# Attention, feed-forward and gated attention: separate PSUM banks for the row maxima of the first batch

## The chip, the cores and the metric

The kernel runs on one core of a Trainium2 chip. Its metric is the device time of one execution in microseconds (us); the kernel before took 964.29 us, the median of three runs (964.15 to 964.66). The profiled execution took 960.93 us, of which 959.20 us are the span from the first instruction to the last.

## The reference

Three stages follow each other on 4 batches of 576 tokens. First a causal attention with 8 heads of 64 and a decay per token:

```
scores = scale * (q @ k.T) + decay;  masked above the diagonal
scores = scores - max(scores, axis=-1)
attn   = exp(scores) / (sum(exp(scores)) + 1e-9)
x      = attn @ v                                   # heads side by side: 576 x 512
```

Then a mixing along the tokens and a feed-forward part with 2048 hidden units:

```
u  = x + (x.T @ U @ V).T
x  = u + relu(u @ w_ch1) @ w_ch2
```

The third stage is attention again, with four experts as heads and a gate that keeps two of them per token. The change lies in the first stage only.

## The kernel before, in words

The eight heads of a batch are worked on in four pairs; 16 pairs in all, numbered 0 to 15 in the code (`p`). The first batch, pairs 0 to 3, has the chip to itself; from pair 4 on (`later_batches`) matmuls of the feed-forward part are put between the attention's by a fixed pattern. A matmul in single precision is made of two or three products of rounded parts.

For each head, `row_max` forms the scores once with rounded operands, in two tiles of two PSUM banks each: `ua` (the last 128 rows, two matmuls) and `ub` (the other rows, four matmuls). VectorE (DVE) reduces both to the maximum of each row (`junk`, `mx`). A small product on TensorE (PE) turns the column `mx` into rows (`mt`), DVE copies it out (`mr`), and two DMAs on SyncE's queue (SP) write it as one more row of the operand `qa`. So `scores` yields differences to the maximum by itself: tile `sc`, two halves of two banks each. ScalarE (ACT) takes the exponential (`pf`) and rounds it (`ph`), DVE forms the rest (`pl`), and `weighted_values` multiplies with the values into one bank (`av`). DVE divides (`den`, `rn`, `x`). The maxima of pair p+1 are formed during pair p.

`value_scale` finds the largest value of a pair through two small products, `amt` and `rsp`. `mix` forms `gp` from the pair's result, ACT and DVE copy it out as `g`, and two products `up` are copied by ACT into `ustage` and sent to memory (`udram`). The feed-forward part loads them again (`ust`), rounds them on ACT (`uh`) and GpSimd (POOL, `ul`), and forms `hps` (hidden) and `cps` (output).

The weights `w1` and `w2` come in tiles: a DMA (`raw`), one step on DVE (L303), one on ACT (L304), two on DVE (L305, L306) into `wst`, then the rounded part on ACT (`w1h`, `w2h`) and the rest on POOL (`w1l`, `w2l`). `load_pair` reads the inputs `qkt` and `vr`; ACT and POOL round them, and SP copies them between partitions.

PSUM has eight banks. Three pools share them: `ps2`, two buffers of two banks (`ua`, `ub` and `sc` take turns in them); `ps1`, one bank (`av`); `psf`, three banks for all small products and the feed-forward products.

What sets the order: from pair 4 on PE's order is the one the code is written in. Everywhere else, and on all other engines, a scheduler orders the instructions before the run from its own estimate of when a buffer comes free; each engine, and SP's queue, then runs its list strictly in that order.

Of the kernel before, what the change touches and what calls it, by code (L numbers as in the profile page):

```python
# [8 lines left out]
F32 = mybir.dt.float32  # L9
# [8 lines left out]
P = 128  # L18
# [4 lines left out]
R = 32  # L23
NP = H // 2
NT = 5
SP_ = 640
HC = 288
# [29 lines left out]
def kernel(  # L57
# [16 lines left out]
    PSUM = bass.MemoryType.PSUM  # L74
# [8 lines left out]
    const = pool("const")  # L83
    dram = pool("dram", space=bass.MemoryType.DRAM)
    ps2 = pool("ps2", 2, space=PSUM)
    ps1 = pool("ps1", 1, space=PSUM)
    psf = pool("psf", 3, space=PSUM)
    small = pool("small", 4)


# [40 lines left out]
    ydram = dram.tile([B, P, KT, S], F32, name="ydram")  # L131
    cdram = dram.tile([B * H, 2, S], F32, name="cdram")

    cur = {}
    counter = [0]


# [10 lines left out]
    def row_max(hb, mx):  # L148


        qa, qb, ka, kb = hb
        ua = ps2.tile([P, 2, 512], F32, name="ua", tag="s2")
        for c0, c1 in ((0, HC), (HC, S)):
            nc.tensor.matmul(ua[:, c0 // HC, 0:HC], qa[0:66, M_LO[4]:S], ka[0:66, c0:c1],
                             start=True, stop=True)
        ub = ps2.tile([P, 2, 512], F32, name="ub", tag="s2")
        where = {3: (0, 0), 0: (0, 448), 2: (1, 0), 1: (1, 320)}
        for t in (3, 2, 1, 0):
            bk, off = where[t]
            w = M_W[t]  # L160
            n = 64 if t == 0 else P
            nc.tensor.matmul(ub[0:n, bk, off:off + w], qa[0:66, M_LO[t]:M_LO[t] + n],  # L162
                             ka[0:66, 0:w], start=True, stop=True)
        junk = cur["att"].tile([P, S], BF16, name="junk", bufs=1)
        nc.vector.tensor_tensor_reduce(
            junk[:].rearrange("p (c n) -> p c n", c=2), ua[:, :, 0:HC],
            maskm[:].rearrange("p (c n) -> p c n", c=2), 1.0, NEG, OP.add, OP.max, mx[:, 4:5])
        for t in (3, 2, 1, 0):
            bk, off = where[t]
            w = M_W[t]  # L170
            n = 64 if t == 0 else P
            m0 = S - P if t == 0 else S - w
            nc.vector.tensor_tensor_reduce(  # L173
                junk[0:n, 0:w], ub[0:n, bk, off:off + w], maskm[0:n, m0:m0 + w], 1.0, NEG,
                OP.add, OP.max, mx[0:n, t:t + 1])
        yield
        mt = psf.tile([NT, P], F32, name="mt", tag="f")
        nc.tensor.transpose(mt[:], mx[:], ident[:])
        mr = small.tile([NT, P], F32R, name="mr", bufs=2)
        nc.vector.tensor_scalar(mr[:], mt[:], PSCALE_LN / ISC, None, OP.subtract)  # L180
        row = f32(qa[66:67, :])
        nc.sync.dma_start(row[:, 0:64], f32(mr[0:1, 0:64]))
        return nc.sync.dma_start(row[:, 64:S].rearrange("o (t p) -> o t p", p=P),
                                 f32(mr[1:NT, :]))
# [59 lines left out]
    def value_scale(vr):  # L244

        am = small.tile([P, 1], F32, name="am")
        nc.vector.tensor_reduce(am[:], vr, AX.XYZ, OP.max, apply_absolute_value=True)
        yield
        at_ = psf.tile([1, P], F32, name="amt", tag="f")
        nc.tensor.transpose(at_[:], am[:], ident[:])  # L250
        ar = small.tile([1, 1], F32, name="ar")
        nc.vector.tensor_reduce(ar[:], at_[:], AX.X, OP.max)
        nc.vector.tensor_scalar(ar[:], ar[:], 1.0e-30, None, OP.max)
        nc.vector.tensor_scalar(ar[:].bitcast(I32), ar[:].bitcast(I32), 0x7F800000, None,
                                OP.bitwise_and)
        yield

        rp = psf.tile([P, 1], F32, name="rsp", tag="f")
        nc.tensor.matmul(rp[:], ones1[:], ar[:].bitcast(BF16)[:, 1:2], start=True, stop=True)
        rs = small.tile([P, 1], F32, name="rs")  # L260
        nc.vector.reciprocal(rs[:], rp[:])
        return rs
# [95 lines left out]

    def ffn_hidden(t, weights, uh, ul):
        w1h, w1l, w2h, w2l = weights  # L360
        ph = psf.tile([P, HC], F32, name="hps", tag="f")
        fs = slice(t * P, t * P + P)
        todo = [(w, uh, k) for k in range(KT) for w in (w1h, w1l)]
        todo += [(w1h, ul, k) for k in range(KT)]
        for n, (wa, xa, k) in enumerate(todo):
            nc.tensor.matmul(ph[:], wa[:, k, fs], xa[:, k, :], start=n == 0,  # L366
                             stop=n == 3 * KT - 1)
        hh = cur["fh"].tile([P, HC], F32R, name="hh")
        hl = cur["fh"].tile([P, HC], F32R, name="hl")
        nc.scalar.activation(hh[:], ph[:], AF.Relu)  # L370
        nc.vector.scalar_tensor_tensor(hl[:], ph[:], 0.0, f32(hh[:]), OP.max, OP.subtract)  # L371
        return hh, hl

    def ffn_out(d, weights, hs, yc):
        w1h, w1l, w2h, w2l = weights
        pc = psf.tile([P, HC], F32, name="cps", tag="f")
        dsl = slice(d * P, d * P + P)
        n = 0
        for t, (hh, hl) in enumerate(hs):
            for wa, xa in ((w2h, hh), (w2l, hh), (w2h, hl)):  # L380
                nc.tensor.matmul(pc[:], wa[:, t, dsl], xa[:], start=n == 0, stop=n == 3 * FT - 1)  # L381
                n += 1
        nc.vector.tensor_tensor(yc[:, d, :], pc[:], yc[:, d, :], OP.add)  # L383
# [158 lines left out]
    def mix(p):  # L542

        b, m, x = p // NP, p % NP, xs[p]
        gp = psf.tile([3 * R, P], F32, name="gp", tag="f")
        for t in range(NT):
            k = 64 if t == NT - 1 else P
            nc.tensor.matmul(gp[:], ut[0:k, t, :], x[0:k, t, :], start=t == 0,  # L548
# [4 lines left out]
        yield  # L553
        ust = sx.tile([P, S], F32, name="ustage")
        for (t0, t1, c0, c1) in ((0, 2, 0, 256), (2, 5, 256, S)):
            up = psf.tile([P, 512], F32, name="up", tag="f")
# [98 lines left out]
    def later_batches():  # L655
# [4 lines left out]
        for p in range(NP, NPAIR):  # L660
# [30 lines left out]
            if p == NP:  # L691
                sin0.release()
                att0.release()
                pre.release()
                cur["fu"] = pool("fu", 2, "right")
                cur["fh"] = pool("fh", 8, "right")
                cur["fy"] = pool("fy", 3, "right")
# [116 lines left out]
    def project(w0, y):  # L814

        yh, yl = y
        for c in range(NC):
            pq = psf.tile([P, HC], F32, name="pq", tag="f")
            cs = slice(c * HC, c * HC + HC)
            n = 0  # L820
            for k in range(KT):
# [33 lines left out]
    def expert_values(b, y):  # L855
# [2 lines left out]
        vr = sy.tile([P, NT, NV], F32, name="vr3", bufs=1)  # L858
        v0 = 2 * E * D
        for t in range(NT):  # L860
            pv = psf.tile([P, 512], F32, name="pv", tag="f")
            ts_ = slice(t * P, t * P + P)
            n = 0
            for k in range(KT):
# [15 lines left out]
    def turn_outputs(b, m, oh, ol):  # L880
# [2 lines left out]
        ms = slice(m * P, m * P + P)  # L883
        for (t0, t1) in ((0, 3), (3, 5)):
            c0, c1 = t0 * P, min(t1 * P, S)
            op = psf.tile([P, 512], F32, name="op", tag="f")
# [8 lines left out]
    def out_products(t, oh, ol, which):  # L895
        k = 64 if t == NT - 1 else P
        ts_ = slice(t * P, t * P + k)
        po = psf.tile([P, 512], F32, name="po", tag="f")
# [68 lines left out]
    with tc.manual_schedule(engines={mybir.EngineType.PE}):  # L967
# [46 lines left out]
                work_on(2 if more else 1)  # L1014
        expert_attend(B - 1, E - 1)
        work_on(100)
    for p_ in (ys[1], sy, att, hpool2, hpool, sy0, sw, small, psf, ps1, ps2, dram, const):
        p_.release()


# [55 lines left out]
```

## Time and profile before

| | |
|---|---|
| median of 3 runs | 964.29 us |
| profiled execution | 960.93 us, span 959.20 us |
| PE busy | 862.3 us (90% of the span) |
| DVE, ACT, POOL busy | 554.7, 416.5, 286.7 us |
| mean granted TensorE clock | 0.944 of full speed |

Busy time is the time in which an engine has an instruction running; the rest is waiting. The profile says for each wait which engine or DMA ended it. The granted clock is 1.00 at 2.4 GHz and 0.50 at 1.2 GHz. A line such as L218 is a line of the kernel before; in the changed kernel the same line stands two further down in the first stage.

### The profile page before, as it was taken

To read this page: it belongs to the slowest core of one execution; us is meant where nothing else is said; L and a number is where in the kernel's file an instruction comes from. 1 tells how busy PE (TensorE), PEld (TensorE's weight loads), DVE (VectorE), ACT (ScalarE), POOL (GpSimd) and SP (SyncE) were. 2 spreads that over 40 slices of the span, in tenths; PEclk is the share of its full clock that TensorE was granted. 3 is DMA by queue.
4 is the path that set the end of the run, shared out by engine and by line. 5 is a ranking of instruction groups with operands and counts; after the bars stand their busy time and mean duration, and the time that the engine had idled before them with its cause. 6 is when DMAs were issued, how large, how long until landed. Compare 5 with 4: busy or idle time off the path is not lost.

```text
span 959.2 us, 19001 instructions
## 1 busy us (share of the span) xinstructions
PE 862.3 (90%) x7480; PEld 804.7 (84%) x7480; DVE 554.7 (58%) x1468; ACT 416.5 (43%) x784; POOL 286.7 (30%) x238
## 2 busy tenths in 40 slices
PE   4887778989999989989999999999999787999987
PEld 3766567888888878989999999999998787888965
DVE  7787677877666555542255652222225566667674
ACT  4556455655445544442134442222113444545454
POOL 8445354443433224021135333323023303001010
PEclk9987568999999999999999999999999787999999
DMA  6434454444533332103168653424006210212201
GB/s 172 136 84 133 146 155 140 120 133 130 138 108 84 104 109 60 52 14 112 50 222 286 217 203 111 149 73 127 28 26 183 65 40 12 75 38 65 49 36 66
DMA packets 68777, 101.94 MB, mean 106 GB/s; under 512 B 6608, under 2 KB 49424, under 8 KB 68688
## 3 DMA queue, kind: packets, MB, share of 16 engines
q1 hardware_dynamic: 64416, 92.47, 32.7%
q10 hardware_dynamic: 4272, 8.26, 2.3%
q8 instruction: 59, 0.97, 0.4%
q14 instruction: 30, 0.25, 0.1%
HBM read 60.33 MB, written 22.56 MB: 86 GB/s over the span
## 4 chain that ended last, share of the span: by engine, by line
PE 67%; DVE 12%; DMA 8%; ACT 6%; issue 4%; POOL 2%; SPq 1%; ACTq 0%; POOLq 0%; DVEq 0%
PE hps L366 19%; PE cps L381 18%; PE sc L209 8%; PE pq L823 4%; PE pv L866 3%; DMA ust<-udram 2%; DVE pl L220 2%; PE po L901 2%; PE av L236 2%; PE gp L548 2%; PE ub L162 2%; ACT pf L218 2%; DVE junk L173 2%; PE av L240 2%; PE av L238 2%
## 5 line engine op out<-in xcount | busy, mean ns | idle before, releaser
L381 PE MATMUL cps<-hh,w2h 128*128 128x288 f32 x512 | 156.3, 306 | 5.6 <-DVE yc L383 3.7
L381 PE MATMUL cps<-hh,w2l 128*128 128x288 f32 x512 | 153.1, 299 | 1.3 <-POOL w2l L341 1.3
L381 PE MATMUL cps<-hl,w2h 128*128 128x288 f32 x512 | 152.2, 297 | 0.0
L220 DVE TENSOR_TENSOR pl<-pf,ph 128x576 f16<-128x576 f32 x144 | 117.7, 823 | 51.8 <-ACT ph L219 51.2
L366 PE MATMUL hps<-uh,w1h 128*128 128x288 f32 x512 | 145.3, 305 | 0.2 <-ACT uh L351 0.2
L366 PE MATMUL hps<-uh,w1l 128*128 128x288 f32 x512 | 141.8, 299 | 0.0
L371 DVE SCALAR_TENSOR_TENSOR hl<-hps,hh 128x288 fp32r<-128x288 f32 x128 | 58.0, 453 | 119.1 <-ACT hh L370 119.0
L370 ACT ACTIVATE hh<-hps 128x288 fp32r<-128x288 f32 x128 | 52.3, 409 | 155.1 <-PE hps L366 154.9
L218 ACT ACTIVATE pf<-sc 128x576 f32<-128x576 f32 x144 | 84.0, 612 | 61.3 <-PE sc L209 55.9
L381 PEld LDWEIGHTS cps<-hh,w2h 128*128 128x128 f32 x512 | 97.9, 191 | 6.5 <-DVE yc L383 4.4
L381 PEld LDWEIGHTS cps<-hh,w2l 128*128 128x128 f32 x512 | 97.9, 191 | 1.5 <-POOL w2l L341 1.5
L366 PEld LDWEIGHTS hps<-uh,w1h 128*128 128x128 f32 x512 | 97.9, 191 | 0.6 <-ACT uh L351 0.4
L366 PEld LDWEIGHTS hps<-uh,w1l 128*128 128x128 f32 x512 | 97.9, 191 | 0.0
L381 PEld LDWEIGHTS cps<-hl,w2h 128*128 128x128 f32 x512 | 97.7, 191 | 0.0
L236 PE MATMUL av<-vh,ph 128*128 128x65 f16 x720 | 91.9, 206 | 1.9 <-DVE x L282 1.6
L366 PE MATMUL hps<-ul,w1h 128*128 128x288 f32 x512 | 89.4, 297 | 4.6 <-POOL ul L352 4.6
L238 PE MATMUL av<-vl,ph 128*128 128x64 f16 x720 | 90.5, 202 | 0.0
L240 PE MATMUL av<-vh,pl 128*128 128x65 f16 x720 | 90.0, 202 | 0.1
L209 PE MATMUL sc<-qa,ka 67*128 67x288 f32 (+4 forms) x288 | 83.0, 348 | 7.9 <-ACT pf L218 3.8
L219 ACT CAST ph<-pf 128x576 f16<-128x576 f32 x144 | 88.3, 638 | 1.6
L236 PEld LDWEIGHTS <-ph 128*128 128x128 f16 x720 | 70.9, 104 | 13.7 <-issue 5.6
L173 DVE CUSTOM_DVE_ANT_0 junk<-ub,maskm 128x448 bf16<-128x448 f32 x192 | 79.6, 414 | 3.2 <-PE ub L162 1.2
(160 smaller groups left out, 1966.1 us busy)
## 6 DMA issues: line engine op xcount, KB each, us to landing
raw<-in_w_dram SPq DMA_DIRECT2D x32, 512.0 KB
ust<-udram SPq DMA_DIRECT2D x22, 576.0 KB
qkt<-in_qk_dram SPq DMA_DIRECT2D x16, 576.0 KB
yc<-ydram SPq DMA_DIRECT2D x14, 576.0 KB
ydram<-yc SPq DMA_DIRECT2D x14, 576.0 KB
vr<-in_v_dram SPq DMA_DIRECT2D x16, 320.0 KB
udram<-ustage ACTq DMA_DIRECT2D x16, 288.0 KB
ydram<-ust SPq DMA_DIRECT2D x8, 576.0 KB
```

Of the source, the lines that this page charges most:

```text
L173: nc.vector.tensor_tensor_reduce(junk[0:n, 0:w], ub[0:n, bk, off:off + w], maskm[0:n, m0:m0 + w], 1.0, NEG, OP.add, OP.max, mx[0:n, t:t + 1])
L209: nc.tensor.matmul(ps[:, bk, off:off + w], wa, xa, start=bk not in banks[:n], stop=bk not in banks[n + 1:])
L218: nc.scalar.activation(pfv, view, AF.Exp, scale=ISC)
L219: nc.scalar.copy(ph[:, o0:o0 + n], pf[:, 0:n])
L220: nc.vector.tensor_tensor(pl[:, o0:o0 + n], pf[:, 0:n], ph[:, o0:o0 + n], OP.subtract)
L236: nc.tensor.matmul(av[0:m, it, :], ph[0:k, c:c + m], vh[0:k, jt, :], start=first, stop=False)
L238: nc.tensor.matmul(av[0:m, it, 0:64], ph[0:k, c:c + m], vl[0:k, jt, :], start=False, stop=False)
L240: nc.tensor.matmul(av[0:m, it, :], pl[0:k, c:c + m], vh[0:k, jt, :], start=False, stop=last)
L366: nc.tensor.matmul(ph[:], wa[:, k, fs], xa[:, k, :], start=n == 0, stop=n == 3 * KT - 1)
L370: nc.scalar.activation(hh[:], ph[:], AF.Relu)
L371: nc.vector.scalar_tensor_tensor(hl[:], ph[:], 0.0, f32(hh[:]), OP.max, OP.subtract)
L381: nc.tensor.matmul(pc[:], wa[:, t, dsl], xa[:], start=n == 0, stop=n == 3 * FT - 1)
```

## The change

The pool `psf` with three banks is replaced, until the middle of pair 4, by two pools: `psm` with one buffer of two banks, which `ua` and `ub` share, and `psg` with one bank, which all small products share. `ps2` is left to the scores alone. In the middle of pair 4 both pools are released, `ua` and `ub` go back to `ps2`, and `psf` is made with three banks as before.

```
+    psm = pool("psm", 1, space=PSUM)
+    psg = pool("psg", 1, space=PSUM)
-    psf = pool("psf", 3, space=PSUM)
...
-    cur = {}
+    cur = {"psm": psm, "psf": psg}
...
-        ua = ps2.tile([P, 2, 512], F32, name="ua", tag="s2")
+        ua = cur["psm"].tile([P, 2, 512], F32, name="ua", tag="s2")
...
-        ub = ps2.tile([P, 2, 512], F32, name="ub", tag="s2")
+        ub = cur["psm"].tile([P, 2, 512], F32, name="ub", tag="s2")
...
-        mt = psf.tile([NT, P], F32, name="mt", tag="f")
+        mt = cur["psf"].tile([NT, P], F32, name="mt", tag="f")
...
                 pre.release()
+                psg.release()
+                psm.release()
+                cur["psm"] = ps2
+                cur["psf"] = pool("psf", 3, space=PSUM)
```

Every other use of `psf` becomes `cur["psf"]` in the same way. No instruction is added or removed; with other buffers the scheduler puts them in another order on every engine.

On PE, at the start of the kernel, the list of the kernel before (`ka0`, `qa0` are the first head of pair 0, `ka1` the second, `ka2` the first head of pair 1):

```order
L154 MATMUL ua_214<-ka0_138,qa0_136 128x288 x2
L162 MATMUL ub_217<-ka0_138,qa0_136 128x448
L162 MATMUL ub_217<-ka0_138,qa0_136 128x320
L162 MATMUL ub_217<-ka0_138,qa0_136 128x192
L162 MATMUL ub_217<-ka0_138,qa0_136 64x64
L154 MATMUL ua_234<-ka1_146,qa1_144 128x288 x2
L178 MATMUL mt_228<-ident_72,mx1_94 5x128
L162 MATMUL ub_237<-ka1_146,qa1_144 128x448
L162 MATMUL ub_237<-ka1_146,qa1_144 128x320
L162 MATMUL ub_237<-ka1_146,qa1_144 128x192
L162 MATMUL ub_237<-ka1_146,qa1_144 64x64
L154 MATMUL ua_312<-ka2_154,qa2_152 128x288 x2
```

The same place in the changed kernel:

```order
L156 MATMUL ua_217<-ka0_141,qa0_139 128x288 x2
L164 MATMUL ub_220<-ka0_141,qa0_139 128x448
L164 MATMUL ub_220<-ka0_141,qa0_139 128x320
L164 MATMUL ub_220<-ka0_141,qa0_139 128x192
L164 MATMUL ub_220<-ka0_141,qa0_139 64x64
L180 MATMUL mt_231<-ident_75,mx1_97 5x128
L156 MATMUL ua_237<-ka1_149,qa1_147 128x288 x2
L164 MATMUL ub_240<-ka1_149,qa1_147 128x448
L164 MATMUL ub_240<-ka1_149,qa1_147 128x320
L164 MATMUL ub_240<-ka1_149,qa1_147 128x192
L164 MATMUL ub_240<-ka1_149,qa1_147 64x64
L211 MATMUL sc_337<-qa0_139,ka0_141 128x288
```

The scores of the first head now stand ahead of the maxima of pair 1 and of the second head's `mt`. From the start of pair 4 on PE's list is the same in both kernels.

On ACT, where the feed-forward part begins (pair 5, `uh`), before:

```order
L340 CAST w2h<-wst 128x512
L219 CAST ph<-pf 128x512
L351 CAST uh<-ust 128x1152
L267 CAST vh_177<-vr 128x10x64
L351 CAST uh<-ust 128x1152
L218 ACTIVATE pf<-sc 128x576
L304 ACTIVATE raw<-raw 128x512
L219 CAST ph<-pf 128x576
L370 ACTIVATE hh<-hps 128x288
L218 ACTIVATE pf<-sc 128x512
L340 CAST w2h<-wst 128x512
L218 ACTIVATE pf<-sc 128x512
```

and in the changed kernel, where one `w2h` has come before already, just ahead of the DMA to `udram`:

```order
L342 CAST w2h<-wst 128x512
L353 CAST uh<-ust 128x1152
L220 ACTIVATE pf<-sc 128x576
L269 CAST vh_180<-vr 128x10x64
L353 CAST uh<-ust 128x1152
L221 CAST ph<-pf 128x576
L306 ACTIVATE raw<-raw 128x512
L372 ACTIVATE hh<-hps 128x288
L497 CAST qa_155<-qkt 64x576
L498 CAST ka_157<-qkt 64x576
L220 ACTIVATE pf<-sc 128x512 x2
L342 CAST w2h<-wst 128x512
```

Two `w2h` instead of one stand ahead of the first `uh`; the two last `pf` no longer have a `w2h` between them, but the casts `qa`, `ka` of a later pair's input ahead of them.

On SP's queue, the loads of `ust` for the same place, before:

```order
L324 DMA raw<-in_w_dram 128x1024 x2
L182 DMA qa_152<-mr 1x16x4
L183 DMA qa_152<-mr 1x4x128
L509 DMA ka_146<-cdram 2x576
L510 DMA qa_144<-qb_145 64x576
L348 DMA ust<-udram 128x4x288 x2
L511 DMA ka_146<-kb_147 64x576
L514 DMA kb_147<-kb_147 64x576
L324 DMA raw<-in_w_dram 128x1024
```

and in the changed kernel:

```order
L326 DMA raw<-in_w_dram 128x1024 x2
L184 DMA qa_155<-mr 1x16x4
L185 DMA qa_155<-mr 1x4x128
L326 DMA raw<-in_w_dram 128x1024
L511 DMA ka_149<-cdram 2x576
L512 DMA qa_147<-qb_148 64x576
L513 DMA ka_149<-kb_150 64x576
L516 DMA kb_150<-kb_150 64x576
L350 DMA ust<-udram 128x4x288 x2
L485 DMA qkt<-in_qk_dram 128x1152
```

The third `w2` tile moved from behind `ust` to ahead of it, and two copies between partitions moved ahead of `ust` too.

## Rows read from the trace of the kernel before

**Rows 1.** Stretches: length, engines' busy time (instructions), granted clock, DMA share, GB/s

```profile
96.00:120.00 24.00, 17.73 (x112) 14.37 (x111) 14.69 (x39) 11.18 (x21) 7.96 (x6) 0.55 0.44 146
144.00:168.00 24.00, 20.43 (x171) 18.34 (x170) 17.43 (x45) 13.33 (x25) 10.79 (x8) 0.84 0.49 141
250.00:740.00 490.00, 473.31 (x3978) 458.47 (x3977) 224.90 (x564) 172.18 (x324) 144.61 (x114) 0.99 0.37 115
```

**Rows 2.** Waits of PE, 0 to 99.5 us: us in total, times, longest

```profile
PE up L557 <- DVE g L552: 5.8, 2, 3.0
PE sc L209 <- ACT pf L218: 3.8, 5, 0.9
...
PE sc L209 <- DVE mx L165: 1.5, 2, 1.2
```

**Rows 3.** Timeline of the first head: start, us, engine, line, operation, count, [wait before]

```profile
11.18 1.05 PE L162 MATMUL ub<-ka,qa 66*128 66x448 f32 x4
...
12.66 0.74 DVE L165 CUSTOM_DVE_ANT_0 junk<-ua,maskm 128x576 bf16<-128x576 f32 x1
```

**Rows 4.** Chain that ended last: an input load; timeline: the second head's scores

```profile
22.88 3.83 DMA qkt<-in_qk_dram
...
26.77 0.59 PE L209 MATMUL sc<-qa,ka 67*128 67x288 f32 x1
```

**Rows 5.** Timeline from the `mix` of pair 2 to pair 4's first scores

```profile
96.31 0.59 PE L178 MATMUL mt<-ident,mx 128*5 128x128 f32 x2
96.42 0.42 ACT L563 COPY ustage<-up 128x320 f32<-128x320 f32 x1 [0.62 <-PE up L560]
96.72 0.49 DVE L180 TENSOR_SCALAR mr<-mt 5x128 fp32r<-5x128 f32 x2 [0.71 <-PE mt L178]
...
99.46 0.58 PE L209 MATMUL sc<-qa,ka 67*128 67x288 f32 x1 [1.09 <-DMA qa<-mr]
```

**Rows 6.** Timeline of PE in the middle of pair 4

```profile
111.94 2.69 PE L548 MATMUL gp<-x,ut 128*96 128x128 f32 x10 [3.16 <-DVE x L282]
...
115.81 0.42 PE L250 MATMUL amt<-ident,am 128*1 128x128 f32 x1
...
117.92 0.41 PE L209 MATMUL sc<-qa,ka 67*128 67x320 f32 x1
```

**Rows 7.** Timeline where the feed-forward part begins: SP and PE

```profile
121.59 1.31 SPq L348 DMA_DIRECT2D ust<-udram  x2
...
122.99 0.58 SPq L511 DMA_DIRECT2D ka<-kb  x1
...
127.35 0.61 PE L366 MATMUL hps<-uh,w1h 128*128 128x288 f32 x1 [0.22 <-ACT uh L351]
```

**Rows 8.** Timeline of the longest wait of PE in pair 5

```profile
137.12 0.62 ACT L340 CAST w2h<-wst 128x512 fp32r<-128x512 f32 x1 [3.65 <-DVE wst L306]
137.65 0.59 ACT L218 ACTIVATE pf<-sc 128x512 f32<-128x512 f32 x1
138.29 1.22 PE L162 MATMUL ub<-ka,qa 66*128 66x448 f32 x4 [3.55 <-ACT pf L218]
```

**Rows 9.** Timeline of the last two `w2` tiles and the products that need them

```profile
149.03 0.62 ACT L340 CAST w2h<-wst 128x512 fp32r<-128x512 f32 x1 [0.61 <-DVE wst L306]
...
156.27 0.62 ACT L340 CAST w2h<-wst 128x512 fp32r<-128x512 f32 x1
...
156.94 0.40 PE L381 MATMUL cps<-hh,w2h 128*128 128x288 f32 x1 [1.84 <-ACT w2h L340]
...
158.60 0.61 PE L381 MATMUL cps<-hh,w2l 128*128 128x288 f32 x1 [1.26 <-POOL w2l L341]
```

**Rows 10.** Timeline: the same four matmuls at the low and the high clock

```profile
159.73 1.05 PE L162 MATMUL ub<-ka,qa 66*128 66x448 f32 x4
...
170.31 0.74 PE L162 MATMUL ub<-ka,qa 66*128 66x448 f32 x4
```

**Rows 11.** Waits of PE, 170 to 260 us: us in total, times, longest

```profile
PE ub L162 <- ACT pf L218: 3.0, 3, 2.0
```

More of the change, by code (lines that the diff above doesn't have):

```diff
@@ L248, in value_scale @@
         yield
-        at_ = psf.tile([1, P], F32, name="amt", tag="f")
+        at_ = cur["psf"].tile([1, P], F32, name="amt", tag="f")
         nc.tensor.transpose(at_[:], am[:], ident[:])
@@ L256, in value_scale @@
         yield
-        rp = psf.tile([P, 1], F32, name="rsp", tag="f")
+        rp = cur["psf"].tile([P, 1], F32, name="rsp", tag="f")
         nc.tensor.matmul(rp[:], ones1[:], ar[:].bitcast(BF16)[:, 1:2], start=True, stop=True)
@@ L360, in ffn_hidden @@
         w1h, w1l, w2h, w2l = weights
-        ph = psf.tile([P, HC], F32, name="hps", tag="f")
+        ph = cur["psf"].tile([P, HC], F32, name="hps", tag="f")
         fs = slice(t * P, t * P + P)
@@ L375, in ffn_out @@
         w1h, w1l, w2h, w2l = weights
-        pc = psf.tile([P, HC], F32, name="cps", tag="f")
+        pc = cur["psf"].tile([P, HC], F32, name="cps", tag="f")
         dsl = slice(d * P, d * P + P)
@@ L544, in mix @@
         b, m, x = p // NP, p % NP, xs[p]
-        gp = psf.tile([3 * R, P], F32, name="gp", tag="f")
+        gp = cur["psf"].tile([3 * R, P], F32, name="gp", tag="f")
         for t in range(NT):
@@ L555, in mix @@
         for (t0, t1, c0, c1) in ((0, 2, 0, 256), (2, 5, 256, S)):
-            up = psf.tile([P, 512], F32, name="up", tag="f")
+            up = cur["psf"].tile([P, 512], F32, name="up", tag="f")
             nc.tensor.matmul(up[:, 0:c1 - c0], g[:], vs[:, c0:c1], start=True, stop=False)
@@ L817, in project @@
         for c in range(NC):
-            pq = psf.tile([P, HC], F32, name="pq", tag="f")
+            pq = cur["psf"].tile([P, HC], F32, name="pq", tag="f")
             cs = slice(c * HC, c * HC + HC)
@@ L860, in expert_values @@
         for t in range(NT):
-            pv = psf.tile([P, 512], F32, name="pv", tag="f")
+            pv = cur["psf"].tile([P, 512], F32, name="pv", tag="f")
             ts_ = slice(t * P, t * P + P)
@@ L885, in turn_outputs @@
             c0, c1 = t0 * P, min(t1 * P, S)
-            op = psf.tile([P, 512], F32, name="op", tag="f")
+            op = cur["psf"].tile([P, 512], F32, name="op", tag="f")
             for t in range(t0, t1):
@@ L897, in out_products @@
         ts_ = slice(t * P, t * P + k)
-        po = psf.tile([P, 512], F32, name="po", tag="f")
+        po = cur["psf"].tile([P, 512], F32, name="po", tag="f")
         todo = [(x, w, m) for m in which for x, w in ((oh, woh), (oh, wol), (ol, woh))]
@@ L1016 @@
         work_on(100)
-    for p_ in (ys[1], sy, att, hpool2, hpool, sy0, sw, small, psf, ps1, ps2, dram, const):
+    for p_ in (ys[1], sy, att, hpool2, hpool, sy0, sw, small, cur["psf"], ps1, ps2, dram, const):
         p_.release()
```

## The prediction

> **What bounds the kernel now.** I read the granted clock first, then the table of stretches, the waits of PE, the chain of waits, and the timeline of the first 180 us. The stretches show where there is anything to win: between 250 and 740 us PE is busy for 473.31 of 490 us at a clock of 0.99, while between 96 and 120 us it is busy for 17.73 of 24 us and the clock is 0.55, that is near the lower of its two levels, 1.2 GHz [rows 1]. The change touches nothing after pair 4, so it can only move the time at which PE reaches its dense part, at about 170 us. What is won or lost before that stays, unless PE arrives early and then waits there for an engine that has not come forward with it.
>
> In the first 99.5 us PE waits in two ways that the PSUM buffers have a part in. The scores wait 3.8 us for ACT's exponential and 1.5 us for DVE's row maxima, because scores and maxima take turns in the same two buffers; and `up` waits 5.8 us for `g`, with PE's strict list offering nothing else to do [rows 2]. After that, two waits are large: 3.55 us for an exponential that stands behind `w2h` on ACT [rows 8], and 1.84 and 1.26 us for the last `w2` tile [rows 9]. The reader should see in these two that the weights, not the attention, are what is late there.
>
> **The change part by part.** It adds and removes no instruction. It exchanges waits for buffers, and it lets the scheduler write other lists. I take the steps in order of time; each is a shift of PE's progress in us, minus for earlier. The sum is made against the profiled execution's own 960.93 us (span 959.20 us), which lies 3.36 us below the median of 964.29 us; the forecast for the median is that median plus the sum.
>
> Scores in pairs 0 to 3, removed. With `ps2` to themselves the two halves of a score need no maxima to be read first, and the next head's first half finds a buffer whose exponential is long done: I count the whole 3.8 + 1.5 = 5.3 us [rows 2]. The 5.8 us before `up` are filled: PE's new list has products `av` between `gp` and `up`, where the old one has only matmuls that come later anyway. But `av` needs `pl` from DVE, the engine that was late with `g`, so I count half, 2.9 us.
>
> Scores in pairs 0 to 3, added. `ub` must now wait until DVE has read `ua`: for the first head it started at 11.18 us, before DVE read `ua` from 12.66 to 13.40 us [rows 3], so 2.2 us. The first scores started only at 19.64 us [rows 3], so most of this is covered. For the other nine heads the wait would be about 0.9 us each (0.74 us for the read and some 0.15 us for the hand-over); in six of them the new list puts `av` or scores between `ua` and `ub`, and the first two overlap the start, so two remain: 1.8 us. The second head's `mt` now stands behind the first head's scores, and its DMA therefore behind a load of inputs that took 3.83 us; that head's scores began at 26.77 us [rows 4], and I add 1.5 us, between 0 and 3.8. On SP's queue another such load moves ahead of the row maxima of pair 3: again 1.5 us between the same ends. Together the lead of PE at pair 4's first scores is 5.3 + 2.9 - 1.8 - 3.0 = 3.4 us. Its ends are 0 (DVE and ACT take all of it) and 5.3 + 5.8 = 11.1 us.
>
> One bank for the small products, in pair 4, where PE's list stays as it was and nothing is put between. Nine products stand there in turn: `mt`, `mt`, `amt`, `rsp` at the start, `gp`, `amt`, `mt`, `up`, `up` in the middle. Before, the two `mt` ran back to back in 0.59 us, right behind `up`; now the first waits for `ustage` (0.42 us) and the second for the first's `mr` (half of 0.49 us) [rows 5]. A hand-over is such a read, 0.25 to 0.42 us, and the way to it and back, which I estimate at 0.3 us from the 0.41 us between the start of `mt` and that of `mr`: about 0.7 us. At the start four of them make 2.8 us, and the four products, at the 0.42 us of `amt` [rows 6], 1.7 us: 4.5 us, against the 3.15 us from `mt` to the scores now (96.31 to 99.46 us, mostly the DMA of `mr`, which still covers that much) [rows 5]. That is 1.4 us. In the middle, from `amt` at 115.81 to the scores at 117.92 us it takes 2.1 us [rows 6]; three hand-overs are added, 2.2 us. Sum 3.6 us, between 1 (only the `ustage` reads show) and 6.3 us (nine times 0.7, nothing covered).
>
> Start of the feed-forward part. `ust` is issued at 121.59 us and `hps` starts at 127.35 us, having waited for it [rows 7]. In the new list the third `w2` tile and two copies of 0.58 us go first: 1.2 us for the issues. The tile's own transfer could add more on the DMA engines; the ends are 0 and 3.8 us, the latter that of a load [rows 4]. So `hps` starts 1.4 us later than before (-3.4 + 3.6 + 1.2).
>
> The wait of 3.55 us in pair 5 [rows 8]. It ended when ACT did the second of two `pf`, after a `w2h`. In the new list both `pf` stand ahead of that `w2h`, but behind two casts for pair 7, which I put at the 0.62 us of the cast in the same rows: 3.55 - 1.24 = 2.3 us earlier, between 0 and 3.55.
>
> The last `w2` tile [rows 9]. Two `w2h` come before the first `uh` instead of one, so the fourth takes the place of the third, 149.03 instead of 156.27 us. That is 7.2 us earlier, and `cps`, which came to it at 155.1 us (156.94 - 1.84), waits for it no more: 1.84 + 1.26 = 3.1 us. Ends 0 and 3.1.
>
> The clock behind that wait. The rows after it ran at the low clock: the four matmuls of `ub` took 1.05 us there and 0.74 us ten us later [rows 10]. Some 6.8 us ran so; at the high clock they would need about 2.0 us less (0.74/1.05 of 6.8 is 4.8). Against it, PE that is earlier meets the exponentials that it waited 3.0 us for further on [rows 11] at most as much earlier. I set the two against each other: 0, between -2.0 and +3.0.
>
> Sum: -3.4 + 3.6 + 1.2 - 2.3 - 3.1 + 0 = -4.0 us, so 956.9 us for an execution like the profiled one, and 964.29 - 4.0 = 960.3 us for the median.
>
> One rule speaks against the change. In pair 4 the granted clock of the stretch from 96 to 120 us is 0.55 already [rows 1]. The Trainium skill, TensorE: Matmul & The Clock Gate, section A second HAM failure mode: psum-queue depth-cycling, says that going through PSUM banks in turn can leave PE so many small pauses that its clock goes up and down and throughput is lost. By that rule the hand-overs would cost clock as well; but here it is near the lower level without them, and what could still be lost is the share by which [rows 10] differ, 0.3 of the 3.6 us, 1.1 us. The sum by the rule would be -2.9 us.
>
> **The rivals.** No change: every small product waits for the read of the one before, with nothing covered, 6.3 instead of 3.6 us. The two `mt` back to back now [rows 5] speak for it, the DMA behind them that takes longer anyway against it. The sum is then -1.3 us: 963.0 us. The Trainium skill, Perfetto Trace Analysis, section Optimizing Tensor Performance, advises independent groups to rotate through different banks so that one is read while the next is computed; by that advice this rival would be the likely one, and the back-to-back pair agrees with it.
>
> Slower: SP's queue. Big loads stand ahead of small copies on which scores wait: at the second head, at pair 3, and ahead of pair 7's casts, which now stand before the two `pf` on ACT. Each costs the full 3.83 us of such a load [rows 4] rather than my 1.5, 1.5 and 0, if the copies land behind the load instead of beside it. All three: -4.0 + 2.3 + 2.3 + 3.8 = +4.4 us, 968.7 us; two of them, one being the last, -4.0 + 2.3 + 3.8 = +2.1 us, 966.4 us. For it speaks that all are issued on one queue; against it that a load lands within 4 us and its copy is needed about 2 us later. It decides from two of the three places on.
>
> Larger gain: DVE is not in the way, `up` counts in full (2.9 more), and the clock stays up (2.0 more): -4.0 - 2.9 - 2.0 = -8.9 us, 955.4 us.
>
> **How the numbers follow.** Forecast 0.50, with a range of its own of 957.4 to 962.3; larger gain 0.07; no change 0.22; slower 0.21. A change of 0.2%, 1.9 us, is about what a measurement of this kernel can tell from none. So faster 0.57, same 0.22, slower 0.21. The range 956.0 to 966.6 leaves out most of the larger gain and the upper half of the slower case, some 0.17.
>
> **What would show it.** Right: pair 4's first scores two to five us before 99.46; no wait of `sc` for ACT's `pf` in pairs 0 to 3; the gap from `amt` to the scores in pair 4 about 4 us instead of 2.1; `hps` within 2 us of 127.35; no wait of `cps` for `w2h` near 155. Wrong: scores of pairs 0 or 3 that wait more than 3 us for `qa`, `pf` in pair 5 that waits for `qkt`, or a `cps` that still waits for its last `w2` tile.

## The result, and the profile after

The changed kernel took 973.81 us, the median of four runs (970.22 to 979.84), against 964.22 us of the kernel before beside it (962.79 to 964.66). The ratio is 1.013, with a 95% interval of 1.0092 to 1.0168: slower by 9.6 us, where 960.3 us had been forecast. The profiled execution took 970.22 us (span 968.5); it is the fastest of the four, so the profile shows the smaller part of the loss.

The stretches of the changed kernel, in the columns of [rows 1]:

```profile
96.00:120.00 24.00, 13.69 (x119) 11.58 (x119) 14.72 (x30) 11.83 (x21) 13.82 (x9) 0.57 0.51 148
120.00:144.00 24.00, 18.41 (x109) 14.54 (x106) 16.29 (x42) 13.16 (x22) 9.56 (x6) 0.50 0.54 170
144.00:168.00 24.00, 22.63 (x192) 20.73 (x193) 20.42 (x44) 14.33 (x29) 12.83 (x9) 0.86 0.35 102
250.00:740.00 490.00, 473.87 (x4012) 458.51 (x4013) 225.73 (x561) 170.45 (x319) 143.68 (x112) 0.99 0.37 115
```

The dense part from 250 us on is as before [rows 1]; what was lost was lost ahead of it. The waits of PE up to pair 4's first scores, which now start at 108.01 us, against [rows 2]:

```profile
PE sc L211 <- DMA qa<-mr: 8.6, 6, 3.3
PE ub L164 <- DVE mx L167: 4.4, 6, 1.0
PE av L240 <- POOL vl L270: 3.8, 1, 3.8
PE av L238 <- DVE x L284: 2.2, 1, 2.2
```

The waits of [rows 2] are gone: no score waits for ACT's exponential or for the maxima, and `up` no longer for `g`. In their place scores wait for the row in `qa` that the maxima make, 8.6 us against 2.7 us before, and `ub` for the reading of `ua`, 4.4 us. DVE, the busiest engine of this stretch, waits too. Its waits in the same 108 us:

```profile
DVE den L275 <- PE av L242: 8.8, 4, 4.6
DVE pl L222 <- ACT ph L221: 5.0, 5, 1.7
DVE junk L175 <- PE ub L164: 3.6, 4, 1.3
...
DVE junk L167 <- PE ua L156: 3.0, 7, 0.8
```

The reductions wait 6.6 us for `ua` and `ub`; before, up to the same point, it was 1.4 us. DVE's work up to there is about the same (74.1 us against 76.4), its idle time went from 23.1 to 33.9 us. PE, which needs `ub` read, and DVE, which needs it computed, take turns. What delays a row is seen at the second head; here is PE's timeline in the changed kernel:

```profile
12.94 1.22 PE L164 MATMUL ub<-ka,qa 66*128 66x448 f32 x4 [0.98 <-DVE mx L167]
16.07 0.38 PE L180 MATMUL mt<-ident,mx 128*5 128x128 f32 x1 [1.92 <-DVE mx L175]
16.28 0.82 PE L156 MATMUL ua<-ka,qa 66*128 66x288 f32 x2
17.96 1.22 PE L164 MATMUL ub<-ka,qa 66*128 66x448 f32 x4 [0.86 <-DVE mx L167]
...
22.57 0.58 PE L211 MATMUL sc<-maskt,identb 128*128 128x64 bf16 x4
22.95 0.42 PE L180 MATMUL mt<-ident,mx 128*5 128x128 f32 x1
...
29.36 0.58 PE L211 MATMUL sc<-qa,ka 67*128 67x288 f32 x1 [3.29 <-DMA qa<-mr]
```

And the same products of the kernel before:

```profile
13.52 0.82 PE L154 MATMUL ua<-ka,qa 66*128 66x288 f32 x2 [1.28 <-DVE mx L165]
...
18.59 0.38 PE L178 MATMUL mt<-ident,mx 128*5 128x128 f32 x1 [1.23 <-DVE mx L173]
```

The second head's `ua` had a buffer at 13.52 us; now it needs the first head's `ub` to be read and starts at 16.28. Its `mt` comes 4.4 us later, and its scores, at 26.77 us before [rows 4], start at 29.36. Two more things go into that. DVE ended these maxima at 21.03 us, against 18.53 before, so the buffer accounts for 2.5 of the 4.4 us; for the other 1.9 us `mt` stands behind the first head's scores, where the new list has it. And the row itself was slow. The end of DVE's maxima, then SP's queue, then two pieces of the chain of waits that ended last, all in the changed kernel:

```profile
20.96 0.07 DVE L175 DVE_READ_ACCUMULATOR2_ANT mx<- 64x1 f32 x1
...
22.93 0.34 SPq L485 DMA_DIRECT2D qkt<-in_qk_dram  x1
23.71 0.55 SPq L184 DMA_DIRECT2D qa<-mr  x1
...
24.31 4.91 DMA qa<-mr
...
36.47 1.68 DMA qa<-mr
```

SP issued the row (L184 and L185, two DMAs) as soon as `mr` was there, but right behind a load of inputs. From the second DMA's issue it took 4.91 us to land, where the third head's took 1.68; the wait of 3.29 us lies in that difference.

The second head is not where most of the time went. The third head's scores start at 38.29 us, only 0.7 us later than before (37.61). Counted by matmuls, PE's 150th starts 0.6 us later than before (43.32 against 42.74 us) and its 300th 5.3 us later (63.77 against 58.49), though the lists do not mix them in quite the same way. The stretch around that, in the kernel before and then in the changed kernel:

```profile
38.00:60.00 22.00, 19.51 (x204) 17.22 (x204) 16.98 (x52) 11.88 (x23) 10.13 (x7) 1.00 0.41 111
```

```profile
38.00:60.00 22.00, 18.54 (x135) 16.18 (x136) 15.66 (x47) 11.76 (x22) 11.59 (x8) 0.58 0.32 84
```

PE is busy for nearly as long and gets through 135 matmuls instead of 204, at a granted clock of 0.58 instead of 1.00. The clock was 1.00 up to 38.1 us; from 25.8 us to there PE had been busy for 7.15 us, where the kernel before had 10.54, and two waits for rows, of 3.29 and 2.04 us, lie there, the second ending at 38.29.

In pair 4 the single bank shows about as forecast. PE before the first scores, against [rows 5], and in the middle of the pair, against [rows 6]:

```profile
103.71 0.27 PE L180 MATMUL mt<-ident,mx 128*5 128x128 f32 x1 [0.52 <-ACT ustage L565]
104.92 0.27 PE L180 MATMUL mt<-ident,mx 128*5 128x128 f32 x1 [0.93 <-DVE mr L182]
105.56 0.27 PE L252 MATMUL amt<-ident,am 128*1 128x128 f32 x1 [0.37 <-DVE mr L182]
107.19 0.16 PE L261 MATMUL rsp<-ar,ones 1*128 1x1 bf16 x1 [1.36 <-DVE ar L256]
108.01 0.58 PE L211 MATMUL sc<-qa,ka 67*128 67x288 f32 x1 [0.65 <-DMA qa<-mr]
...
125.77 0.42 PE L252 MATMUL amt<-ident,am 128*1 128x128 f32 x1
126.56 0.38 PE L180 MATMUL mt<-ident,mx 128*5 128x128 f32 x1 [0.37 <-DVE ar L254]
...
130.07 0.63 PE L211 MATMUL sc<-qa,ka 67*128 67x320 f32 x1
...
140.93 0.61 PE L368 MATMUL hps<-uh,w1h 128*128 128x288 f32 x1 [1.26 <-ACT uh L353]
...
151.06 0.63 PE L164 MATMUL ub<-ka,qa 66*128 66x448 f32 x4
...
164.13 0.38 PE L383 MATMUL cps<-hh,w2h 128*128 128x288 f32 x1
```

From `mt` to the scores it takes 4.3 us (3.15 before), from `amt` to the scores 4.3 (2.1 before). The last two rows answer to [rows 8, 9]: `ub` and `cps` no longer wait.

### The profile page after: what moved, and what is told of

Its sections match the earlier page's. It is cut to its first block, busy times and chain, and to the rows that moved or that the text cites. A ratio compares the mean times of both kernels' runs of the same rounds, so it can differ in the third digit from the quotient of the medians.

```text
span 968.5 us, 18989 instructions
## 1 busy us (share of the span) xinstructions
PE 863.3 (89%) x7480; PEld 803.1 (83%) x7480; DVE 555.3 (57%) x1468; ACT 416.8 (43%) x784; POOL 290.9 (30%) x238
## 4 chain that ended last, share of the span: by engine, by line
PE 65%; DVE 14%; DMA 8%; ACT 6%; POOL 3%; issue 3%; SPq 1%; ACTq 0%; POOLq 0%; DVEq 0%
PE hps L368 17%; PE cps L383 17%; PE sc L211 8%; PE pq L829 4%; PE pv L872 3%; DMA ust<-udram 3%; PE po L907 2%; PE gp L550 2%; PE av L238 2%; DVE pl L222 2%; DVE junk L175 2%; PE ub L164 2%; ACT pf L220 2%; PE av L242 2%; PE av L240 2%
## 5 line engine op out<-in xcount | busy, mean ns | idle before, releaser
L222 DVE TENSOR_TENSOR pl<-pf,ph 128x576 f16<-128x576 f32 x144 | 115.2, 806 | 45.0 <-ACT ph L221 44.3
```

The lines of the kernel that those rows point to most:

```text
L222: nc.vector.tensor_tensor(pl[:, o0:o0 + n], pf[:, 0:n], ph[:, o0:o0 + n], OP.subtract)
```

## The experiments

Four theories were put to the test. B: the one bank for small products costs the time. M: the maxima lost by having one buffer of their own where they had two in turn. L: the lists that the scheduler wrote for the new banks cost it. C: small waits keep TensorE's clock low, and that is the cost. The table gives, for every run, the median, the ratio to the kernel before on the same chip with its interval, and of the profiled execution the start of pair 4's first scores and of the first `hps` (99.46 and 127.35 us before, 108.01 and 140.93 in the changed kernel).

| run | scores and maxima | small products | lists | median us | ratio (95%) | scores, pair 4 | `hps` |
|---|---|---|---|---|---|---|---|
| e1 | 2 + 1 buffers | 1 bank | before | 977.45 | 1.0137 (1.0097 to 1.0177) | 114.76 | 144.29 |
| e2 | 2 shared | 1 | before | 972.41 | 1.0105 (1.0074 to 1.0136) | 111.74 | 141.22 |
| e3 | 2 + 1 | 1 | after, SP's before | 1007.85 | 1.0466 (1.0406 to 1.0526) | 127.06 | 160.31 |
| e4 | 2 + 1, to pair 3 | 1, to pair 3 | own | 975.77 | 1.0107 (1.0058 to 1.0157) | 110.09 | 141.12 |
| e5 | 2 shared | 2 | before | 963.04 | 0.9996 (0.9970 to 1.0023) | 100.84 | 129.28 |
| e6 | 2 shared | 2, filled | before | 959.55 | 0.9965 (0.9933 to 0.9997) | 96.87 | 124.79 |
| e7 | 2 shared | 1, filled | before | 969.15 | 1.0056 (1.0035 to 1.0076) | 103.55 | 132.67 |
| e8 | 2 shared | 3, filled | before | 962.86 | 1.0001 (0.9975 to 1.0028) | 96.64 | 124.80 |
| e9 | 2 shared | 1 | own | 974.72 | 1.0114 (1.0062 to 1.0167) | 106.43 | 138.40 |
| e10 | 2 shared | 2 | own | 965.10 | 1.0019 (0.9983 to 1.0055) | 99.09 | 127.78 |
| e11 | 2 + 1 | 2 with `av` | own | 974.69 | 1.0135 (1.0078 to 1.0193) | 104.44 | 134.55 |
| e12 | 2 shared | 2, `av` 2 | own | 963.45 | 1.0004 (0.9974 to 1.0034) | 95.86 | 126.57 |
| e13 | 3 shared | 2 with `av` | own | 970.12 | 1.0090 (1.0050 to 1.0130) | 98.87 | 129.21 |
| e14 | 3 shared | 1 | own | 976.41 | 1.0139 (1.0106 to 1.0172) | 106.86 | 137.43 |
| e15 | 2 + 1 | 1, filled | after | 969.04 | 1.0060 (1.0042 to 1.0078) | 108.21 | 140.84 |

"2 + 1" is two buffers for the scores and one for the maxima, as in the changed kernel; "2 shared" is the kernel before. All of it holds for the first batch alone. "Lists" says whose order the engines run: that of the kernel before, that of the changed kernel, or the one that the scheduler wrote for the run itself. The ratios are the measure across runs; a start comes from one execution each.

**The new banks with the old lists (e1).** The order of the instructions on all five engines is written out as a table, traced instruction by traced instruction, and tied in that order:

```
+    for eng, text in ORDER.items():            # ORDER: the lists of the kernel before
...
+        for a, z in zip(seq, seq[1:]):
+            tc.add_manual_dep(of[z], of[a].name, ...NoSync...)
```

> The PSUM banks are those of the changed kernel; the order of the instructions on all five engines is written out and is that of the kernel before, word for word. Theory L (the lists): what the changed kernel lost, 9.6 us, came from the lists that the scheduler wrote for the new banks, so this run stays within 4 us of before (at most 968.5 us), and pair 4's first scores start within 4 us of 99.46 us. Theory B (the banks): the waits for the one small bank and for the two-bank buffer of the maxima are the loss, whatever the order; then it is 971 us or more, and pair 4's first scores start at 105 us or later.

Theory L falls as the cause of the loss: with the old lists the new banks cost no less than with the new ones, and pair 4's first scores come later still.

**One small bank alone (e2), and with its own lists (e9).**

```
-    psf = pool("psf", 3, space=PSUM)
+    psg = pool("psg", 1, space=PSUM)           # ua, ub stay in ps2
```

> Only the small products get one bank in the first batch; the maxima share the two score buffers as before, two banks stay empty, and the order on all engines is that of the kernel before. It prices the one bank alone, over pairs 0 to 4. Theory B1 (the one bank is the loss): 970 us or more, with waits of mt, amt, rsp, gp and up for reads that sum to 6 us or more before pair 4's first scores. Theory L (the lists): plus 2 to 4 us, 966 to 968.5 us, of which 1 to 4 us in the middle of pair 4.

> One small bank in the first batch, maxima in the score buffers, two banks empty, and now the lists that the scheduler writes for it. With the lists of the kernel before it took 972.4 us. Theory 1 (the one bank is the whole loss of the change, and the maxima's own banks bring nothing): 971 to 975 us, like the changed kernel. Theory 2 (the lists of before did not suit one bank): 966 us or less, and then the maxima's own banks, the other half of the change, cost the rest.

The one bank by itself costs 1.0 to 1.1%, nearly as much as the whole change (1.3%), whichever list it has. How it does that is less clear. The profile of e2, whose list is that of the kernel before, is of the slowest of its nine executions (978.68 us, median 972.41). Both stretches run from the start to pair 4's first scores; first the kernel before, then e2:

```profile
0.00:99.46 99.46, 69.93 (x582) 59.73 (x583) 76.39 (x209) 54.66 (x98) 55.29 (x68) 0.90 0.46 132
```

```profile
0.00:111.74 111.74, 78.03 (x583) 65.92 (x583) 76.15 (x209) 55.07 (x97) 54.65 (x68) 0.74 0.41 118
```

The same matmuls keep PE busy 8.1 us longer, at a mean granted clock of 0.74 instead of 0.90, and PE is idle 4.2 us longer (33.7 against 29.5; the 2.6 us in e5's expectation are too few). The first of the new small waits, of `amt` for `mr`, and a wait ahead of it, in e2:

```profile
32.06 0.73 PE L260 MATMUL sc<-qa,ka 67*128 67x320 f32 x3 [1.79 <-ACT pf L269]
...
33.85 0.42 PE L229 MATMUL mt<-ident,mx 128*5 128x128 f32 x1
36.01 0.37 PE L301 MATMUL amt<-ident,am 128*1 128x128 f32 x1 [1.74 <-DVE mr L231]
```

The granted clock is 0.69 between 24 and 48 us and 0.60 between 48 and 72, where the kernel before had 1.00 and 0.88. But it fell at 33.0 us, behind the wait of 1.79 us for ACT's exponential, which the kernel before has with 0.92 us, and ahead of the wait of `amt`: that the small waits took the clock down is not shown. In e2, e4, e9 and e14 PE is busy for 77.7 to 80.1 us up to pair 4's first scores. The changed kernel and e1 are busy for 70.8 and 73.7 and idle for longer instead (37.2 and 41.1 us). e4 has the banks of the changed kernel up to there; its profile has PE busy for 80.1 us and idle for 30.0, and reaches the place 2.1 us later. So one execution spends as busy time at a low clock about what the other spends waiting.

**Two small banks (e5, e10, e12).** As e2, with `pool("psg", 2, ...)`; e10 with the scheduler's own lists; e12 gives the bank left over to a second `av`.

> As the run with one small bank (maxima in the score buffers, every list that of the kernel before), but the small products have two banks in the first batch; one bank stays empty. In that run TensorE reached pair 4's first scores 12.3 us later than before, of which only 2.6 us were more waiting; the rest was the same matmuls at the low clock. Theory C (small waits between matmuls take the clock down, and that is most of the loss): two banks let mt and amt run back to back again, so the clock rises as in the kernel before and the time is within 3 us of it (961 to 965 us). Theory W (the hand-over itself is the loss, in proportion to the banks): about half of the one-bank loss of 11 us remains, 966 to 968 us.

> Two small banks, maxima in the score buffers, one bank empty, with the lists that the scheduler writes for it. With the lists of before it equalled the kernel before (ratio 0.9996). Expected by both theories: 960 to 966 us; if it is 968 us or more, the scheduler's lists are a cause of their own.

> Two small banks, and the bank that is then left over goes to a second av in the first batch; maxima in the score buffers; the scheduler's lists. If VectorE's waits for av (5.2 us up to pair 4 in the kernel before) come from the one av bank, 2 to 4 us faster than before, 957 to 961 us; if av's bank is no limit, 961 to 966 us.

The step from three banks to two costs nothing that these runs can tell, the step from two to one costs 1.1% with the old lists (e2) and 1.0% with the scheduler's (e9). A second bank for `av` brings nothing that shows in the time. This settles theory B, but not C: e5 met the time that C foretold and not the clock. Between 24 and 96 us its granted clock is 0.79, 0.68 and 0.71 in steps of 24 us, not far from e2's 0.69, 0.60 and 0.68 and far from the 1.00, 0.88 and 0.78 of the kernel before, whose time it has. It fell to 0.50 between 33 and 36 us there too.

**The old banks one pair earlier (e4).** The release stands ahead of pair 4's first scores instead of behind its second `up`.

> The changed kernel, but the old banks come back one pair earlier, before the first scores of pair 4 instead of behind its second up. It takes the one bank out of pair 4 and leaves pairs 0 to 3 as they are in the changed kernel. By the trace of the changed kernel the loss up to pair 4's first scores is 8.5 us and from there to the first hps another 5.1 us; if those 5.1 us are the one bank (4.8 forecast for bank and copy together), this run gives back 3 to 5 us: 969 to 971 us, with hps at about 136 us instead of 140.9. If the one bank in pair 4 costs nothing there, 973 us or more.

The time did not come back: the median is 975.77 us where 969 to 971 had been expected, though the interval of the ratio overlaps that of the changed kernel. PE in the middle of pair 4, in e4:

```profile
126.79 0.42 PE L252 MATMUL amt<-ident,am 128*1 128x128 f32 x1
127.00 0.42 PE L180 MATMUL mt<-ident,mx 128*5 128x128 f32 x1
...
128.98 0.63 PE L211 MATMUL sc<-qa,ka 67*128 67x320 f32 x1
...
141.12 0.61 PE L368 MATMUL hps<-uh,w1h 128*128 128x288 f32 x1 [2.90 <-ACT uh L353]
```

`amt` to scores takes 2.2 us again, so these hand-overs did cost the 2.2 us of the forecast; but `hps` then waits 2.90 us for `uh`. From pair 4's first scores to `hps` it takes 31.0 us, against 32.9 in the changed kernel and 27.9 in the kernel before: 1.9 of the 5.0 us came back, and the later start of pair 4 took them away again. In pair 4 the one bank is a real wait, but not what most of the loss hangs on.

**The rival of the prediction: SP's queue (e3).** The changed kernel with SP's list of the kernel before.

> The changed kernel, with its own lists on TensorE, VectorE, ScalarE and GpSimd, but with SP's list of the kernel before: the row copies stand in their old places among the input loads. Theory S (SP's queue, the rival of the prediction): the 8.6 us that scores wait for the rows in qa shrink to 3 us or less, pair 4's first scores start at 103 us or earlier instead of 108.0, and the time falls to 969 us or less. Theories without SP's queue: 972 us or more, and the wait for qa stays at 6 us or more.

The scores' wait for `qa` did shrink, to 2.6 us up to 160 us, but the run lost 34 us more: `ub` waits 11.1 us for DVE, `rsp` 8.9, `mt` 7.9. One engine's list from another kernel holds up what the other lists expect early, so the time of this run does not test the queue. Its second head does, since up to there only SP's order differs from the changed kernel:

```profile
23.47 0.42 PE L230 MATMUL mt<-ident,mx 128*5 128x128 f32 x1
...
24.23 0.54 SPq L234 DMA_DIRECT2D qa<-mr  x1
...
26.60 0.58 PE L261 MATMUL sc<-qa,ka 67*128 67x288 f32 x1
```

`mt` starts 0.5 us later than in the changed kernel, the row is issued ahead of the loads instead of behind them, and the scores start 2.8 us earlier, without a wait. So the rival is right at the second head: there the copy did land behind the load. It does not make up the loss, since e1, with SP's old list, loses as much, and since the third head of the changed kernel is only 0.7 us late. Whether the slow rows, by way of the clock that fell behind them, cost more than that was not tried.

**The maxima's own buffer (e11, e13, e14).** In e11 the small products and `av` take two banks together, and the maxima keep their own buffer. In e13 the same six banks serve scores and maxima as three buffers in turn; e14 does that with one small bank.

```
-    ps2 = pool("ps2", 2, space=PSUM)
-    psm = pool("psm", 1, space=PSUM)
+    psm = pool("psm", 3, space=PSUM)            # ua, ub and sc (e13, e14)
```

> The changed kernel with the maxima in two banks of their own, but the small products and av together have two banks instead of one each, with the lists that the scheduler writes for it. Theory 1 (the one small bank is the loss): a second bank is there for small products when av is not in work, so half or more of the loss comes back, 963 to 969 us. Theory M (the one buffer of the maxima, in which ub waits for ua's read and the next ua for ub's, makes the rows late): still 971 us or more, and the wait of scores for the rows in qa stays at 5 us or more up to pair 4.

> As the run with the maxima's own buffer and two banks for small products and av together (974.7 us), but the same six banks serve scores and maxima as three buffers in turn, instead of two for the scores and one for the maxima. Theory M (the maxima lost by having one buffer of their own where they had two in turn): the next head's ua no longer waits for the reading of ub, the rows come early again, the wait for qa up to pair 4 falls from 7.1 to 3 us or less, and the run takes 960 to 967 us. If sharing av's bank with the small products is the loss: 972 us or more.

> The banks of the changed kernel, one for small products and one for av, but six banks serve scores and maxima as three buffers in turn. If the one small bank is a sufficient cause (one small bank alone, with two buffers in turn: 974.7 us with the scheduler's lists), 970 to 976 us; if it cost only because of the maxima's private buffer, 966 us or less.

PE's waits up to pair 4's first scores, in e11 and then in e13:

```profile
PE sc L210 <- DMA qa<-mr: 7.1, 4, 3.0
PE ub L163 <- DVE mx L166: 5.8, 7, 1.1
```

```profile
PE sc L209 <- DMA qa<-mr: 2.3, 2, 2.0
PE ub L162 <- DVE mx L173: 1.2, 1, 1.2
```

Theory M holds up to there: with three buffers in turn the second head's `mt` starts at 18.28 us instead of 22.78, and pair 4's scores 5.6 us earlier, before those of the kernel before. The small products waited 1.2 us for each other's readers in e11. But each of the two runs has lists of its own: in e13 SP issues the second head's row at 19.35 us, ahead of the loads, in e11 at 23.65 behind them, and there it takes 5.0 us to land. So the 5.6 us are not the buffer's alone. e1 and e2 have the same lists and one small bank each, and differ in nothing but the maxima's buffer: pair 4's scores start 3.0 us later with the private buffer (114.76 against 111.74), and all four executions of e1 (976.31 to 979.70 us) lie above seven of e2's nine. That is the cleanest price of the private buffer here. With the scheduler's lists no whole time shows it by itself: the intervals of e11 and e13 overlap, e11 and e10 (1.0019) lie apart but differ in `av`'s bank too, and the two causes do not add up, since e14, without the private buffer, is no faster than the changed kernel. A private buffer beside two small banks and an `av` bank of its own would need nine banks, so e11 has `av` share, and what that sharing costs was not tried alone. The end of e13 missed the expected 960 to 967 us: after `hps` it loses what it had kept, at one place in pair 5:

```profile
151.29 0.53 PE L548 MATMUL gp<-x,ut 128*96 128x128 f32 x1 [6.00 <-DVE x L282]
```

Why its lists put `x` so late there was not tried.

**Filling the waits (e6, e7, e8, e15).** Products that nobody reads stand where PE waits: 38 at 17 places of the first 112 us in an empty bank (e6, e7), or 34 and 18 written into the tile that the waiting product starts afresh (e8, e15; in e15 before the scores of the second head of pair 0, of both heads of pair 1, the first of pairs 2 and 4, and `gp` of pair 3; the 37 and 19 of the expectations are miscounts).

```
+    for _ in range(38):                        # e6, e7
+        warm.append(nc.tensor.matmul(wt[:], identb[:], maskm[:, 0:512], start=True,
+                                     stop=True).ins)
```

> The run with two small banks, and in the bank that stays empty 37 products of no use (bf16, 128x128 by 512 columns, read by nobody) at 17 places of the first 112 us where TensorE waits in the kernel before, 1 to 8 at each. Theory C: the fill keeps the clock up, the matmuls between need up to half the time, and the run beats before: 952 to 958 us. Theory W: the fill only takes time, plus 0 to 5 us.

> The run with one small bank and the same fill of 37 products in an empty bank. Theory C: the loss of the one bank was clock, so with the clock held up it falls from 11 us to the waits alone, 3 to 5 us more than the filled run with two banks, and the run is 6 us or more below the unfilled 972.4. Theory W: no gain, 971 us or more.

> The kernel before, its banks and its lists, with 34 products of no use at five places where TensorE waits for an operand and not for a bank (before the first scores of pairs 2 and 4, before two of up and before gp of pair 3); they write into the tile that the waiting product starts afresh. Theory C: the clock, 0.55 to 0.88 between 48 and 144 us before, is higher there, and the run is 2 to 6 us faster than before. Theory W: 0 to 3 us slower.

> The changed kernel, its banks and its lists, with 19 products of no use before six products that wait there (the scores of both heads of pairs 0 and 1, the first scores of pairs 2 and 4 and gp of pair 3; they write into the tile that the waiting product starts afresh). Theory C (a large part of the loss is the clock): 4 us or more faster than the changed kernel, 970 us or less, with a higher clock between 24 and 144 us than 0.86, 0.72, 0.86, 0.57, 0.50. Theory of waits alone (VectorE's maxima come late, and a faster TensorE only waits longer): within 3 us of 973.8 us.

Against the unfilled run the ratio falls by 0.3% with two banks (e5 to e6), 0.5% with one (e2 to e7), nothing with three (e8), and 0.7% in the changed kernel (1.013 to e15's 1.006); only the last pair has intervals that do not overlap. In e8 the clock rose as expected, to 1.00 between 48 and 72 us, and the time did not move. One bank costs 0.9% against two when both are filled and 1.1% when neither is. So filling these waits does not do away with most of the loss between one and two banks; the small waits between `mt` and `amt` were not filled, and what they cost in clock stays open. In e15 the profiled execution reaches the first scores of pair 4 at 108.21 us and `hps` at 140.84, as the changed kernel does. The higher clock that theory C wanted did not come: 0.84, 0.71, 0.67, 0.62 and 0.57 in the five stretches from 24 to 144 us, against 0.86, 0.72, 0.86, 0.57 and 0.50. So e15 meets the time that C foretold without its sign, and why it is faster stays open. Its four runs lie within 0.3 us (968.94 to 969.22), those of the changed kernel within 9.6; the gain is to the median, and 1.2 us to the changed kernel's fastest run. e6 is the one version faster than the kernel before, by 0.35%, with an interval that ends just below 1; one such among fifteen can be chance.

## Why the prediction was wrong

**The lead in pairs 0 to 3 is the step that failed.** It was -3.4 us, between 0 and -11.1, and measured +8.55 (99.46 to 108.01), outside its ends. The removals came: 3.8 + 1.5 us are gone, and all of the 5.8 before `up`, of which half had been counted. The additions, set at 1.8 + 1.5 + 1.5 = 4.8 us, were mis-sized. `ub` waits 4.4 us, at six heads and not at two, where 1.8 had been set; rows cost 5.9 us more (8.6 against 2.7), not 3.0; and 6.0 us of waits of `av` for `vl` and `x` were not in the sum at all, which had `av` wait for `pl`. Two thoughts behind it were wrong. I took the maxima's "own banks" as a gain for the scores with one price, the reading of `ua`; but where they had taken turns in two buffers they now had one, and e1 against e2, with the same lists, shows that this moves pair 4 by 3.0 us. And I priced the single small bank in pair 4 only; e2 and e9 reach that pair's first scores 12.3 and 7.0 us late. The end "DVE and ACT take all of it" was set at 0, as if an engine that is 77% busy (76.4 of 99.5 us) could only keep a lead from growing; made to wait in turn with PE it falls behind.

**One bank in pair 4 and `ust`, +3.6 and +1.2, together +4.8:** measured 5.0 (`hps` 13.58 us late, the scores 8.55). The middle was right to the tenth, 2.2 us. That the whole came out is luck in part: PE is busy 2.4 us longer there with the same matmuls (24.16 against 21.72 us), at a clock of 0.50 against 0.56, which the sum had at nothing; and with the one bank taken away e4 got back 1.9 us, since `uh` is then waited for.

**The wait for `pf`, -2.3, and the last `w2` tile, -3.1:** both happened. From `hps` to pair 5's `gp` it took 16.6 us instead of 19.3, -2.8; to the `ua` behind `cps` 24.9 instead of 31.9, another -4.2. Then 2.7 us were given back; on the way `gp` waits 3.0 us for `x` between 138 and 190 us, where it waited 0.6 us between 125 and 180 before. The end is 9.3 us late in the profiles: 8.55 + 5.03 - 2.79 - 4.23 + 2.74.

**The clock, 0 between -2 and +3:** in the profiled execution the busy time up to pair 4 grew by 0.8 us only (70.8 against 69.9), but that is a balance: 0.58 against 1.00 between 38 and 60 us, where PE fell behind, and 0.86 against 0.78 between 72 and 96. I had looked at the clock behind pair 4, where it is low anyway, and not at pairs 1 and 2, where it was high and could be lost. How much of the loss is the clock these runs do not settle: e5 has a low clock there and loses nothing. The rule that I weighed, the Trainium skill, TensorE: Matmul & The Clock Gate, section A second HAM failure mode: psum-queue depth-cycling, agrees with e2 in that 8.1 of 12.3 us are the same matmuls taking longer, at 0.74 instead of 0.90; I had priced it at 1.1 us. That small pauses between products began it is not shown, since the clock of e2 fell at 33.0 us, ahead of the first such wait of `amt`.

**The rivals.** "No change" named the right suspect, the single bank, and priced it in pair 4 alone, 6.3 instead of 3.6 us. The advice beside it, the Trainium skill, Perfetto Trace Analysis, section Optimizing Tensor Performance, to let independent groups rotate through different banks, agrees with e5 and e2: two banks to rotate are enough, one is not. "Slower: SP's queue" gave 966.4 to 968.7 us and was right at one of its three places: the second head's scores waited 3.3 us for `qa`, which I had named as a sign of it, the row landed 4.91 us after its issue behind a load, and in e3, with SP's old order, that wait is gone. At pair 3 a row was slow too (3.8 us), but its scores waited only 0.4. By itself the second head is a small part of the loss, since the third is 0.7 us late.

## What to carry to other kernels

When buffers are split between two users, count for each user how many it can have in flight before and after: a private buffer is a loss where two were shared in turn. Price such a change first where the clock is high and the engines are tied to each other most closely, not where a list is easy to read. Look also at where small copies stand among the loads on a queue, since a late product can slip its copy behind one. And where two engines hand small tiles back and forth, try two banks before giving a third: in this kernel the second was worth 1.1% and the third nothing that could be measured.

## What the runs showed that was not expected

- The banks' cost is a step, not a slope: three to two banks 0.9996 (0.9970 to 1.0023), one bank 1.0105 (1.0074 to 1.0136).
- A higher granted clock alone bought nothing, and a lower one cost nothing: e8 ran at 1.00 between 48 and 72 us, e5 at 0.68, the kernel before at 0.88, and the ratios to it are 1.0001 and 0.9996.
- A row of 2.0 KB took 4.91 us to land right behind a load of 576 KB, and 1.68 us in the same kernel at the next head.
- A step of DVE on a 128x512 tile (L307 in the changed kernel) took 3.13 us at 146.12 and 0.69 us at 157.40. What lay beside it was not varied.
